# Attention and a gated feed-forward layer on one core: first loads and scores by pairs of heads, wider first products for half of batch 0, a last copy in two halves

## The chip, the cores and the metric

The kernel runs on one core of a Trainium2 chip. The metric is the time of one execution on the device in microseconds (us), lower being better. A core has five engines that work side by side and wait for each other by semaphores: TensorE (PE, matrix products; PEld is its loading of weights), ScalarE (ACT, functions element by element), VectorE (DVE), GpSimd (POOL, which here issues the loads) and SyncE (SP, which issues stores). Loads go to SBUF, the on-chip memory; products are written to PSUM, from where ACT and DVE read them.

## The reference

```python
# q, k, v: batch 8, heads 12, sequence 448, head dimension 64
scores = (1.0 / np.sqrt(64)) * np.matmul(q, k.transpose(0, 1, 3, 2))
scores = scores - np.max(scores, axis=-1, keepdims=True)
attn = np.exp(scores)
attn = attn / (np.sum(attn, axis=-1, keepdims=True) + 1e-09)
attn_out = np.matmul(attn, v).astype(np.float32)
x = attn_out.transpose(0, 2, 1, 3).reshape(3584, 768)
h = x @ w_in                              # w_in: 768 x 2048
g = h * (1.0 / (1.0 + np.exp(-h)))
out = (g @ w_out).astype(np.float32)      # w_out: 2048 x 768
```

So each of the 96 heads gives attention over 448 tokens, and the 3584 rows of 768 that come out go through two products with a gate between them.

## The kernel before

**Work and its tiling.** The heads of a batch are taken in three groups of four; a *unit* is one batch and one group, 24 in all, and units 0 to 2 are batch 0. A unit's keys and queries are loaded with partition = 32 x head + token block (`load_k` L314, `load_q` L319) and turned on DVE into the layout that PE wants (`turn_k` L375 with three transpositions, `turn_q` L392). Scores (`scores` L449, `score` L438) are products with 32 rows of PE for each head, so that the four heads of a unit run on PE's four groups of rows at once. They land in PSUM tiles `s`, each for two heads (y = 0 or 1), of which there are three. ACT exponentiates each tile (`expo` L479; L483 for the first two bursts of unit 0, L494 for all others). A unit's scores come in three or four *bursts*; each burst is two exponentials of 896 columns. Value products (L544, L558) and sums of exponentials give the attention, which is scaled on DVE into `xT` (L650, L661).

**The feed-forward layer.** First products `h` = `w_in` x `xT` (`ffn1` L684, all products in `times` L673), one block of 128 of the 2048 inner columns at a time, then a tanh on ACT (L705) and the gate on DVE (L740, L749). For batch 0 the first products are made in two pieces of 224 tokens (PIECES), two blocks sharing a PSUM tile. Second products `o` and `p` follow, for most tiles in a scheme with seven products instead of eight (`product` L910, `combine_g` L895); copies on ACT (`take_copy` L976) and sums on DVE (`take_sum` L981) bring them to SBUF, and `store` (L956) sends them out.

**What sets the order.** Nothing on the engines decides it: a planner in the kernel (`Order` L111, and the loop at L1880) plays the engines through with a cost for each operation and writes the instructions of every engine in the order that it finds. Its inputs are estimates: of products (`mm` L30), of ACT (`act` L34), of loads (L197 to L208, with an extra `DMA_SLOW` for one load). `qk_seq` (L1599) lists the score bursts in order, `qk_at` (L1620) says when the next may run, `run_qk` (L1644) places it; `av_seq` lists the value products; `moe` lists the feed-forward products, which fill PE in between. Before the first of those, idle time of PE is filled with products on zeros (`run_zeros` L1867): an opening run of FIRST = 47 columns-of-128, then shorter ones. POOL issues loads in the order of L1039 to L1066: keys of unit 0, queries of unit 0 in two pieces of columns, keys and queries of unit 1, keys of unit 2, V of batch 0, and so on. A buffer ring holds them back: there are two tiles for keys, so that the keys of unit 2 wait for the turn of unit 0's. An issue also waits until the eighth load before it has landed.

The lines of the order that matter here:

```python
plan_k(0, 0)
plan_q(0)
plan_k(0, 1)
plan_q(1)
plan_k(0, 2)
plan_v(0, 0, NG)
```

Of the kernel before, what the change touches and what calls it, by code (L numbers as in the profile page):

```python
# [18 lines left out]
PE_OUT = 0.20  # L19
# [91 lines left out]
class Order:  # L111
# [48 lines left out]
    def step(self):  # L160
# [26 lines left out]
        elif self.pool:  # L187
# [9 lines left out]
            if at is not None and at <= self.now:  # L197
# [5 lines left out]
                took += DMA_SLOW if len(self.sent) == 3 else 0.0  # L203
                few = len(self.sent) < 7
# [10 lines left out]
def kernel(  # L215
# [27 lines left out]
    PACE = 2.6  # L243
    NPL = 4
# [3 lines left out]
    COLD, FIRST, QUIET = 8.5, 47, 0.16  # L248
# [65 lines left out]
    def load_k(b, hg):  # L314
        t = sb.tile([128, TPP * D], FP16, name=f"rk_{b}_{hg}", tag="rk", bufs=NRK)
        nc.gpsimd.dma_start(out=t, in_=group_of(k, b, hg))
        rawk[(b, hg)] = t

    def load_q(n, g0, g1):  # L319
        b, hg = units[n][:2]  # L320
        if g0 == 0:
            rawq[n] = sb.tile([128, TPP * D], FP16, name=f"rq_{n}", tag="rq", bufs=NRQ)
        cols = slice(D * g0, D * g1)
        nc.gpsimd.dma_start(out=rawq[n][:, cols], in_=group_of(q, b, hg)[:, cols])  # L324
# [50 lines left out]
    def turn_k(b, hg):  # L375
        t = rawk[(b, hg)][:].bitcast(FP32).rearrange("p (g i) -> p g i", i=32)
        kt = sb.tile([128, TPP, 32, 2], FP16, name=f"KT_{b}_{hg}", tag="KT", bufs=3)
        KT[(b, hg)] = kt
        pairs = kt.rearrange("p g i e -> p (g i e)").bitcast(FP32)
# [3 lines left out]
        for x in (0, 2):  # L383
# [4 lines left out]
            if count == 4:  # L388
                lone = 12 * (not high)
                nc.vector.transpose(out=pairs[:, lone : lone + 2], in_=toks[:, :, 3 - 3 * at])  # L390

    def turn_q(n, g0, g1):  # L392
        t = rawq[n][:].bitcast(FP32).rearrange("p (g i) -> p g i", i=32)[:, g0:g1]
# [55 lines left out]
    def scores(n, w, ys):  # L449
        score_banks(n, w, ys)  # L450
        for c, q0, q1, at in strips_of(n, w):
            for e in range(2):
                for h in range(HG):
# [230 lines left out]
    def ffn1(b, f, t0, t1, strips, c0, c1):  # L684
        i = f % blocks(b)
# [13 lines left out]
    def blocks(b):  # L699
        return 2 if b == 0 else 1  # L700

    def tanh(b, f, t0, t1):
        n = (t1 - t0) * blocks(b)
# [30 lines left out]
    def gate(b, f, t0, t1):  # L734
        r = b % 2
        cut = 6 * 128 - S if b == 1 else S
        for lo, hi, dst, at in ((0, cut, G, S * r), (cut, S, X, -cut)):
            lo, hi = max(lo, t0), min(hi, t1)
            if b == 0 and lo < hi:
# [236 lines left out]
    def take_copy(qd, m):  # L976
        nc.scalar.copy(out=ost(qd, *OUT[m]), in_=bank(qd, BANK[m]))  # L977
        if m == 4:
            store(qd, *OUT[m])
# [25 lines left out]
    def plan_q(n):  # L1005
        ld_q[n] = [
            od.load(
                128,
                2 * D * (g1 - g0),
                lambda g0=g0, g1=g1: load_q(n, g0, g1),  # L1010
                None if g0 else rq_ring,
            )
            for g0, g1 in (PIECES if n == 0 else ((0, TPP),))
        ]
# [24 lines left out]
    plan_k(0, 0)  # L1039
    plan_q(0)  # L1040
# [35 lines left out]

    def plan_turn(n):
        b, hg, g0, g1 = units[n]
        if b == B - 1 and not rq_ring.can(1, od.now):
            return False  # L1080
        if (b, hg) not in kt_op:
            if not kt_ring.can(1, od.now):
# [4 lines left out]
                    "DVE", 0.73, lambda: turn_k(b, hg), [ld_k[(b, hg)]], 20, then=rk_ring.give  # L1087
                )
            )
        if b == B - 1:  # L1090
            rq_ring.take()
        qt_op[n] = [
# [3 lines left out]
                    0.13 + (g1 - g0) / 30.0,  # L1096
                    lambda g0=g0, g1=g1: turn_q(n, g0, g1),
                    [load],
                    20,
                    then=rq_ring.give if b == B - 1 else None,  # L1100
                )
            )
            for load, (g0, g1) in zip(ld_q[n], PIECES if n == 0 else ((0, TPP),))
        ]
        return True
# [32 lines left out]
    def gates_at(t, f):  # L1138
# [3 lines left out]
        for b in {(128 * t + c) // S for c in (0, 127)}:  # L1142
            x = g_op.get((b, f), [])
            made += x if len(x) >= (len(PIECES) if b == 0 else 1) else [None]
        return made

    def queue_ffn1(b, g0, g1):
        t0, t1, parts = 32 * g0, 32 * g1, []
        begun = {}
        for f in range(NFF) if b == 0 else [x for f in range(HF if b < PB else FILL) for x in (f, f + HF)]:  # L1150

          half = 6 if b else NDC
          for c0 in range(0, NDC, half):

            def run(f=f, c0=c0):
                c1 = c0 + half
                strips = b > 0 and od.mode == "cols" and bool(qk_seq or av_seq)
                op = Op("PE", half * mm(t1 - t0), lambda: ffn1(b, f, t0, t1, strips, c0, c1), tail=PE_OUT)
                if warm["on"]:
                    warm["on"] = False  # L1160
                n = blocks(b)
# [27 lines left out]
            def deps(f=f, c0=c0):  # L1189
                if c0:  # L1190
                    return [] if begun.get(f) == c0 else [None]
                if f % blocks(b) and f - 1 not in parts:
# [776 lines left out]
```

## Time and profile before

| | |
|---|---|
| three timed runs | 380.28, 380.77, 381.61 us; median 380.77 |
| the profiled execution | 380.37 us |
| its span (first to last instruction) | 378.6 us, so 1.8 us lie around it |
| PE busy, share of the span | 372.4 us, 98% |
| DVE, ACT, POOL busy | 269.7, 255.5, 84.9 us |
| granted clock of PE | full speed throughout |
| exponentials of 896 columns (L494) | 164, mean 923 ns |
| first products of 224 columns | 180 + 11 records, of 192 |
| last copy (L977, 128x384) | starts at 374.73, 0.48 us |

The profile is of one execution. Times inside it are microseconds from its first instruction. A group of rows in the timeline reads: start, duration, engine, line, operation, output<-inputs, shape, how many, and in brackets how long the engine sat idle before it and what ended that. In the chain of waits each row is a stretch of the path that ended last. A few records of products are missing from the trace. In the listing of loads "us to landing" is from issue to landing.

### The profile page before, as it was taken

The numbers are of one execution on the slowest core, as the hardware profiler recorded it, in microseconds if no ns is written. First come the engines' busy times: TensorE is split into PE (matmuls) and PEld (weight loads), VectorE is DVE, ScalarE is ACT, GpSimd is POOL, SyncE is SP. The second block draws the span as 40 slices with busy tenths as digits, with TensorE's granted clock in tenths as the row PEclk, the third lists the DMA queues.
The fourth block names the chain that finished last, engine by engine and source line by source line (L and its number), as shares of the span: only waits on it lengthen the run. The fifth ranks groups of instructions, "written<-read, shape, count | busy, mean of one in ns | idle before, by whom it ended". The sixth has DMA issues, their size and how long they took to land.

```text
span 378.6 us, 9949 instructions
## 1 busy us (share of the span) xinstructions
PE 372.4 (98%) x4024; PEld 191.5 (51%) x4024; DVE 269.7 (71%) x553; ACT 255.5 (67%) x400; POOL 84.9 (22%) x155
## 2 busy tenths in 40 slices
PE   7999999999999999999999999999999999999995
PEld 3367664444444444444444454545555555556663
DVE  3666859899995869995969998898475424446541
ACT  4988874897768787877788777658872238882221
POOL 6652438451007326006423200000000000000000
PEclk9999999999999999999999999999999999999999
DMA  7999999946139948148955421200002331002343
GB/s 120 191 208 210 206 204 186 190 53 98 17 92 124 184 49 124 26 94 116 170 86 73 54 53 34 68 18 0 3 1 59 94 74 26 0 2 59 84 110 83
DMA packets 35854, 34.47 MB, mean 91 GB/s; under 512 B 11872, under 2 KB 35040, under 8 KB 35808
## 3 DMA queue, kind: packets, MB, share of 16 engines
q0 software_dynamic: 25312, 22.82, 40.3%
q1 hardware_dynamic: 10080, 10.53, 10.6%
q8 instruction: 31, 0.51, 0.5%
q10 hardware_dynamic: 416, 0.49, 0.4%
q14 instruction: 15, 0.12, 0.1%
HBM read 45.61 MB, written 11.01 MB: 150 GB/s over the span
## 4 chain that ended last, share of the span: by engine, by line
PE 97%; DMA 1%; ACT 1%; DVE 0%; issue 0%; POOLq 0%
PE p L673 32%; PE h L673 21%; PE f L673 16%; PE s L438 12%; PE a L558 8%; PE o L673 3%; PE a L544 2%; PE a L591 2%; DMA rk<-in_k_dram 1%; ACT T L483 1%; PE z L1872 0%; PE z L673 0%; PE z L544 0%; DVE KT L387 0%; ACT ost L977 0%
## 5 line engine op out<-in xcount | busy, mean ns | idle before, releaser
L494 ACT ACTIVATE E<-s 128x896 f16<-128x896 f32 x164 | 142.0, 923 | 23.7 <-PE s L438 23.6
L673 PEld LDWEIGHTS <-w_in_t 128*128 128x128 f16 (+1 forms) x981 | 61.3, 97 | 45.2 <-issue 8.4
L673 PE MATMUL h<-xT,w_in_t 128*32 128x448 f16 (+2 forms) x834 | 84.0, 333 | 0.0
L344 POOL DMA_DIRECT2D V<-in_v_dram x88 | 48.4, 557 | 52.5 <-PE a L558 32.2
L673 PEld LDWEIGHTS <-G 128*128 128x128 f16 (+1 forms) x637 | 43.4, 97 | 32.4 <-issue 5.2
L977 ACT COPY ost<-p 128x384 f32<-128x384 f32 x52 | 24.9, 479 | 50.4 <-PE p L673 31.9
L705 ACT ACTIVATE th<-h 128x448 f16<-128x448 f32 x67 | 36.6, 546 | 22.8 <-PE h L673 19.1
L673 PE MATMUL p<-w_out_t,G 128*128 128x384 f16 (+1 forms) x343 | 51.9, 326 | 0.0
L438 PE MATMUL s<-rq,KT 32*128 32x448 f16 (+3 forms) x728 | 45.4, 347 | 1.3 <-DVE rq L402 1.0
L983 DVE TENSOR_TENSOR ost<-p,ost 128x384 f32<-128x384 f32 x39 | 21.6, 553 | 31.3 <-PE p L673 14.3
L673 PEld LDWEIGHTS <-S 128*128 128x128 f16 (+1 forms) x330 | 29.5, 98 | 23.5 <-issue 4.2
L673 PE MATMUL p<-D,S 128*128 128x384 f16 (+1 forms) x214 | 37.5, 326 | 0.0
L558 PE MATMUL a<-E,V 128*32 128x448 f16 (+1 forms) x640 | 32.9, 356 | 0.0
L749 DVE SCALAR_TENSOR_TENSOR G<-th,h 128x448 f16<-128x448 f16 (+1 forms) x52 | 28.8, 565 | 4.5 <-ACT th L705 3.9
L324 POOL DMA_DIRECT2D rq<-in_q_dram x25 | 13.8, 553 | 67.3 <-PE s L438 57.7
L661 DVE SCALAR_TENSOR_TENSOR xT<-a,rdn 128x448 f16<-128x448 f32 x46 | 27.0, 618 | 2.7 <-PE a L558 2.0
L438 PEld LDWEIGHTS <-KT 32*128 32x128 f16 (+1 forms) x824 | 12.5, 96 | 30.3 <-issue 28.1
L507 DVE TENSOR_TENSOR T<-T,E 128x1792 f16<-128x1792 f16 x20 | 21.7, 1086 | 3.9 <-ACT E L494 3.8
L876 DVE TENSOR_TENSOR p<-f,p 128x448 f32<-128x448 f32 x15 | 9.4, 624 | 20.4 <-PE f L673 13.5
L673 PE MATMUL f<-sx,tw 128*128 128x448 f16 x102 | 23.5, 352 | 0.0
L507 DVE TENSOR_TENSOR T<-E,E 128x1792 f16<-128x1792 f16 x20 | 21.6, 1082 | 2.5 <-ACT E L494 2.5
L558 PEld LDWEIGHTS <-V 128*32 128x32 f16 (+1 forms) x640 | 13.7, 95 | 18.0 <-issue 10.3
(95 smaller groups left out, 430.2 us busy)
## 6 DMA issues: line engine op xcount, KB each, us to landing
out_dram<-ost SPq DMA_DIRECT2D x194, 48.0 KB, 1.6
rk<-in_k_dram POOLq DMA_DIRECT2D x24, 224.0 KB, 5.0
rq<-in_q_dram POOLq DMA_DIRECT2D x23, 224.0 KB, 5.6
w_out_t<-in_moe_w_out_dram POOLq DMA_DIRECT2D x4, 768.0 KB, 12.5
V<-in_v_dram POOLq DMA_DIRECT2D x42, 64.0 KB, 4.1
V<-in_v_dram POOLq DMA_DIRECT2D x42, 48.0 KB, 4.3
w_in_t<-in_moe_w_in_dram POOLq DMA_DIRECT2D x6, 256.0 KB, 9.0
w_in_t<-in_moe_w_in_dram POOLq DMA_DIRECT2D x3, 512.0 KB, 12.3
```

The costliest lines, as they stand in the source:

```text
L324: nc.gpsimd.dma_start(out=rawq[n][:, cols], in_=group_of(q, b, hg)[:, cols])
L344: nc.gpsimd.dma_start(out=VT[b][32 * x : 32 * (x + 1), hs, at : at + count, :], in_=v[b, hs].rearrange("h (i g) d -> i h g d", g=TPP)[:, : ...
L438: nc.tensor.matmul(out=pS[p0 : p0 + 32 * (x1 - x0), h % 2, at : at + q1 - q0], lhsT=KT[(b, hg)][32 * h : 32 * (h + 1), key_rows(b, hg, c, ...
L494: nc.scalar.activation(out=E[(n, w)][:, 2 * y : 2 * y + 2, :], in_=pS_t[(n, w, y)][:, :, 0:S], func=AF.Exp, scale=attn_scale,)
L507: nc.vector.tensor_tensor(out=T[n], in0=T[n] if step else E[(n, 0)], in1=E[(n, step + 1)], op=ALU.add,)
L558: nc.tensor.matmul(out=a[32 * h : 32 * (h + 1), 0:S], lhsT=VT[b][k0:k1, HG * hg + h, place(b, hg, c), part - 1 :: 2], rhs=e[k0:k1, h], sta ...
L661: nc.vector.scalar_tensor_tensor(out=x3(b, cc)[:, cc % 3, 32 * g0 : 32 * g1], in0=acc[(n, part)][:, 0:nq], scalar=0.5, in1=rdn_t[n].rearra ...
L673: nc.tensor.matmul(out=out[i : i + cut], lhsT=w[:, i : i + cut], rhs=x, start=start, stop=stop, skip_group_check=True,)
L705: nc.scalar.activation(out=th, in_=h_t[(b, f, t0)][:, 0:n], func=AF.Tanh)
L749: nc.vector.scalar_tensor_tensor(out=dst[:, f, at + lo : at + hi], in0=th_t[(b, f, t0)][:, lo - t0 : hi - t0], scalar=1.0, in1=h_t[(b, f, ...
L977: nc.scalar.copy(out=ost(qd, *OUT[m]), in_=bank(qd, BANK[m]))
L983: nc.vector.tensor_tensor(out=t, in0=bank(qd, BANK[m]), in1=t, op=ALU.add)
```

## The change

Four edits, and a few constants of the planner.

- **Loads by pairs of heads.** Keys and queries of unit 0 come in halves of 64 partitions: keys of heads 0 and 1, queries of heads 0 and 1, keys of heads 2 and 3, queries of heads 2 and 3. Before, the keys came whole and the queries in two halves of the columns. One load is added. The turns on DVE go the same way: three operations and two query pieces for each pair of heads.
- **Scores likewise.** The first three bursts of unit 0 are split: all three for heads 0 and 1, then all three for heads 2 and 3. Each half burst is eight products on two of PE's four groups of rows.
- **Half of batch 0's first products 448 wide.** Blocks 0 to 7 stay in two pieces of 224 tokens, two blocks to a PSUM tile; blocks 8 to 15 are made in one piece of 448, one block to a tile. 96 products of 224 become 48 of 448.
- **The last copy by two engines.** Of the last tile of 384 columns ACT copies the first 192 and DVE the other 192.
- **The planner.** The extra for a slow load falls on the fourth load and no longer on the third; the opening run of dummies is 40 columns-of-128 for 47; turns for units 1 to 3 are urgent; a first product costs at least 0.0972. In `turn_k` one transposition is emitted last of the three where it was second.

The built order follows from the planner. In it, unit 0's first value product stands behind the last scores of unit 1 (it stood between unit 1's second and last scores), with dummy products of 1024 columns in its old place. First products and second products of batches 0 and 1 are shifted against the scores. From the scores of unit 11 on, about 110 us in the trace of before, PE has the same order as before. DVE's half of the last copy waits on ACT's semaphore, at the count that ACT's half sets.

The core of the diff:

```diff
-                took += DMA_SLOW if len(self.sent) == 3 else 0.0
-                few = len(self.sent) < 7
+                took += DMA_SLOW if len(self.sent) == 4 else 0.0
+                few = len(self.sent) < 8
...
+    BF0 = 8
...
-    COLD, FIRST, QUIET = 8.5, 47, 0.16
+    COLD, FIRST, QUIET = 8.5, 40, 0.16
...
-    def load_k(b, hg):
-        t = sb.tile([128, TPP * D], FP16, name=f"rk_{b}_{hg}", tag="rk", bufs=NRK)
-        nc.gpsimd.dma_start(out=t, in_=group_of(k, b, hg))
-        rawk[(b, hg)] = t
-
-    def load_q(n, g0, g1):
+    def load_k(b, hg, h0=0, h1=HG):
+        if h0 == 0:
+            rawk[(b, hg)] = sb.tile([128, TPP * D], FP16, name=f"rk_{b}_{hg}", tag="rk", bufs=NRK)
+        rows = slice(32 * h0, 32 * h1)
+        nc.gpsimd.dma_start(out=rawk[(b, hg)][rows], in_=group_of(k, b, hg)[rows])
+
+    def load_q(n, h0=0, h1=HG):
...
-        if g0 == 0:
+        if h0 == 0:
...
-        cols = slice(D * g0, D * g1)
-        nc.gpsimd.dma_start(out=rawq[n][:, cols], in_=group_of(q, b, hg)[:, cols])
+        rows = slice(32 * h0, 32 * h1)
+        nc.gpsimd.dma_start(out=rawq[n][rows], in_=group_of(q, b, hg)[rows])
...
-                nc.vector.transpose(out=pairs[:, lone : lone + 2], in_=toks[:, :, 3 - 3 * at])
-
-    def turn_q(n, g0, g1):
-        t = rawq[n][:].bitcast(FP32).rearrange("p (g i) -> p g i", i=32)[:, g0:g1]
+                lone = pairs[:, lone : lone + 2], toks[:, :, 3 - 3 * at]
+        nc.vector.transpose(out=lone[0], in_=lone[1])
+
+    def turn_q(n, g0, g1, h0=0, h1=HG):
+        rows = slice(32 * h0, 32 * h1)
+        t = rawq[n][rows].bitcast(FP32).rearrange("p (g i) -> p g i", i=32)[:, g0:g1]
...
-                for h in range(HG):
+                for h in [2 * y + i for y in ys for i in range(2)]:
...
-    def blocks(b):
-        return 2 if b == 0 else 1
+    def blocks(b, f):
+        return 2 if b == 0 and f < BF0 else 1
...
-        n = (t1 - t0) * blocks(b)
+        n = (t1 - t0) * blocks(b, f)
...
-        nc.scalar.copy(out=ost(qd, *OUT[m]), in_=bank(qd, BANK[m]))
+        t, p = ost(qd, *OUT[m]), bank(qd, BANK[m])
+        if (qd, m) == (LAST, 4):
+            nc.scalar.copy(out=t[:, 0 : OH // 2], in_=p[:, 0 : OH // 2])
+            nc.vector.tensor_copy(out=t[:, OH // 2 : OH], in_=p[:, OH // 2 : OH])
+        else:
+            nc.scalar.copy(out=t, in_=p)
...
-    plan_k(0, 0)
-    plan_q(0)
+    first_ld = {}
+    for i in range(2):
+        for fn, ring, x in ((load_k, rk_ring, (0, 0)), (load_q, rq_ring, (0,))):
+            first_ld[(i, fn)] = od.load(
+                64,
+                2 * D * TPP,
+                lambda fn=fn, x=x, i=i: fn(*x, 2 * i, 2 * i + 2),
+                None if i else ring,
+            )
...
+    def turn_bias(n):
+        return -11 if n <= 3 else 20
+
...
+        if n == 0:
+            plan_first_turns()
...
-                    "DVE", 0.73, lambda: turn_k(b, hg), [ld_k[(b, hg)]], 20, then=rk_ring.give
+                    "DVE", 0.73, lambda: turn_k(b, hg), [ld_k[(b, hg)]], turn_bias(n), then=rk_ring.give
...
+        if n:
+            plan_turn_q(n)
+        return True
+
+    def plan_turn_q(n):
...
-                    0.13 + (g1 - g0) / 30.0,
-                    lambda g0=g0, g1=g1: turn_q(n, g0, g1),
-                    [load],
-                    20,
-                    then=rq_ring.give if b == B - 1 else None,
+                    0.13 + TPP / 30.0,
+                    lambda: turn_q(n, 0, TPP),
+                    ld_q[n],
+                    turn_bias(n),
+                    then=rq_ring.give if units[n][0] == B - 1 else None,
...
-            for load, (g0, g1) in zip(ld_q[n], PIECES if n == 0 else ((0, TPP),))
...
-        return True
+
+    def plan_first_turns():
+        kt_ring.take()
+        for i in range(2):
+            heads = (2 * i, 2 * i + 2)
+            fn = lambda heads=heads: turn_k(0, 0, *heads)
+            then = rk_ring.give if i else None
+            kt_op[("half", i)] = od.add(
+                Op("DVE", 0.73, fn, [first_ld[(i, load_k)]], 18 + i, then=then)
+            )
+            for x, (g0, g1) in enumerate(PIECES):
+                fn = lambda heads=heads, g0=g0, g1=g1: turn_q(0, g0, g1, *heads)
+                op = Op("DVE", 0.13 + (g1 - g0) / 30.0, fn, [first_ld[(i, load_q)]], 18 + i)
+                qt_op[("half", i, x)] = od.add(op)
+        kt_op[(0, 0)] = kt_op[("half", 1)]
+        qt_op[0] = [qt_op[("half", i, x)] for i in range(2) for x in range(2)]
...
-            made += x if len(x) >= (len(PIECES) if b == 0 else 1) else [None]
+            made += x if len(x) >= blocks(b, f) else [None]
...
-        for f in range(NFF) if b == 0 else [x for f in range(HF if b < PB else FILL) for x in (f, f + HF)]:
+        for f in range(BF0 * (g1 - g0 == TPP), NFF if g1 - g0 == TPP else BF0) if b == 0 else [x for f in range(HF if b < PB else FILL) for x in (f, f + HF)]:
...
-                qk_seq += [([n], w, (0, 1)) for w in range(len(BURSTS[n]))]
+                if n == 0:
+                    qk_seq += [([0], w, (y,)) for y in range(2) for w in range(3)]
+                    qk_seq.append(([0], 3, (0, 1)))
+                else:
+                    qk_seq += [([n], w, (0, 1)) for w in range(len(BURSTS[n]))]
...
-            for x in {0 if c == NCH - 1 else i for c, i in BURSTS[n][c]} if n == 0 and c < 2 else ():
-                turns = [kt_op.get(units[0][:2]), *qt_op.get(0, [None] * 2)[x : x + 1]]
+            if n == 0 and c < NCH - 1:
+                y = ys[0]
+                turns = [kt_op.get(("half", y))]
+                turns += [qt_op.get(("half", y, x)) for x in {i for _, i in BURSTS[0][c]}]
```

## The prediction

> **What bounds the kernel now.** I read the page first, then the chain of waits of the first 80 us, then the timeline of the first 24 us engine by engine, then the end. The page says which engine it is:
>
> ```profile
> span 378.6 us, 9949 instructions
> PE 372.4 (98%) x4024; PEld 191.5 (51%) x4024; DVE 269.7 (71%) x553; ACT 255.5 (67%) x400; POOL 84.9 (22%) x155
> PE 97%; DMA 1%; ACT 1%; DVE 0%; issue 0%; POOLq 0%
> ```
>
> TensorE (PE) is busy 98% of the span and the chain lies on it for 97%. Only the first microseconds and the last four are anybody else's. But "busy" counts the dummy products on zeros and products that stand waiting inside a group, so the first 24 us need the timeline. The chain of waits opens so:
>
> ```profile
> 1.25 3.77 DMA rk<-in_k_dram
> ...
> 5.55 0.26 DVE KT L387
> 5.81 0.30 DVE rq L402
> 6.11 0.04 issue
> 6.15 0.63 PE s L438 x16
> 6.78 2.52 ACT T L483 x3
> ```
>
> The reader sees a start bound by one load: all keys of unit 0 land at 5.02, are turned on DVE, half the queries after them, and the first exponential starts at 6.76. Then the timeline, PE and ACT rows picked out:
>
> ```profile
> 9.85 0.65 DVE L402 STREAM_TRANSPOSE rq<-rq 128x448 f32<-128x448 f32 x1 [0.34 <-DMA rq<-in_q_dram]
> 9.97 9.86 ACT L494 ACTIVATE E<-s 128x896 f16<-128x896 f32 x12
> ...
> 13.96 0.82 PE L438 MATMUL s<-rq,KT 32*128 32x448 f16 x8
> 14.71 0.56 PE L544 MATMUL a<-T,V 128*32 128x448 f16 x8
> ...
> 15.58 0.81 PE L438 MATMUL s<-rq,KT 32*128 32x448 f16 x8
> 16.33 0.56 PE L544 MATMUL a<-T,V 128*32 128x448 f16 x8
> ...
> 17.28 0.74 PE L438 MATMUL s<-rq,KT 32*128 32x224 f16 x16
> ...
> 20.34 2.53 ACT L494 ACTIVATE E<-s 128x896 f16<-128x896 f32 x3 [0.51 <-PE s L438]
> ```
>
> ACT runs without a gap from 6.76 to 19.83, one exponential each 0.80 us. Up to about 17 us ACT sets the pace: the scores of unit 1 (13.96, 15.58) follow each other by two exponentials, 1.6 us, and the 0.87 us between them is filled with a value product (14.71). From 17.28 the roles change: PE has no gap, and ACT waits for it (0.51 at 20.34). After 24 us the groups on PE follow without any stall, and past 110 us the changed program has the same order on every engine but the last copy. So **what counts is when PE gets through unit 2's scores, how much PE work follows, and the last copy.** The end:
>
> ```profile
> 374.73 0.48 ACT L977 COPY ost<-p 128x384 f32<-128x384 f32 x1 [4.72 <-PE p L673]
> 375.24 0.50 ACTq L970 DMA_DIRECT2D out_dram<-ost  x1
> ```
>
> **The change part by part.**
>
> *First exponential.* Landings before: keys 5.02 (issued 1.25, 3.77), first query piece 5.5 (1.93 + 3.6), second 6.9 (2.47 + 4.4), next keys 8.7 (2.99 + 5.7), next queries 9.8 (3.51 + 6.3), then 10.9. A load of 224 KB thus takes 1.1 us of the stream, one of 112 KB about 0.5. After: the first half of the keys lands near 4.5, that of the queries near 5.0. The key turn (three operations, 5.04 to 5.81) takes 0.76, a query piece 0.37; rows are not columns, so 64 partitions take as long. Queries turned at 5.6, scores 0.6 (6.15 to 6.76 before), **first exponential near 6.15: 0.6 earlier.** The scores of a pair of heads use half of PE's rows, so eight products take as long (0.5) as sixteen did: 1.5 us more PE for unit 0. It is covered: before 12.3 us PE held 41 dummy columns-of-128 between the scores, now 29. DVE gets five operations more (about 1.5 us) and has 3.4 idle of the 7 us from 5 to 12. The second half has to give exponential 4 at 6.15 + 3 x 0.80 = 8.55; with queries landing at 6.9, turned at 7.3, scored by 7.95, it does.
>
> *What is late next.* Exponential 7 (11.56 before) needs the queries of unit 1: landing 9.83, turned 9.85 to 10.50. The bytes ahead of them are the same. Scores of 64 rows from 10.55, two rounds of 0.19 and some 0.2 until ACT starts: 11.15, where the chain alone would allow 10.95. So of 0.6 only **0.4** is left. Bounds: 0.62, if that load comes 0.2 earlier; -0.1, if the extra DMA issue costs a half load's 0.5. I keep 0.41, since the stream moves the same bytes.
>
> *POOL.* Keys of unit 2 wait for the second key turn: issued near 7.0 instead of 6.10, the four V loads behind them 0.8 later. Loads from there on take 4.8 to 6.1 us to land where the first took 3.8, so they queue behind data, and this is hidden; without that cover V would come 0.8 later, and its first reader now stands 1.2 us later.
>
> *The moved value product.* The order of the changed program puts unit 0's first value product (14.71 before) behind unit 1's last scores; dummies fill its place. ACT still sets when those scores may run: 16.33 less 0.41. Then both value products (0.87 each) must pass before unit 2's scores. PE loses 0.87; it regains 0.09 (scores at 17.28 waited for a query turn) and 0.16 (group of 0.67 that needs 0.51). **Front: +0.87 - 0.25 - 0.41 = +0.2** (0.0 to +0.7). PE is the bound from there, so it stays.
>
> *First products 448 wide.* In the chain, 30 products of 224 take 2.98 and 24 take 2.41: 0.095 each; 12 of 448 take 2.38, of which 0.11 is the change of form: 0.189. So 96 x 0.0958 - 48 x 0.189 = 0.12; the mean of all 224 pitches, 0.097, gives 0.24. I take **-0.15**. Tanh and gates stay as many and as long.
>
> *Forms.* From unit 2's first scores to the point where the orders meet PE changes form 77 times before, 75 after. Eight scores take 0.505 where two rounds need 0.38, a group of first products 0.106 over its products: 0.11 each, **-0.22** (0 to -0.25).
>
> *Last copy.* The built order shows VectorE's half waiting for ACT's half. A copy of 384 takes 0.479, of 448 about 0.53, so 192 on ACT 0.33; VectorE's half from its sum of 384 (0.558) and its 224 against 448 columns (0.417, 0.62) 0.36; from one to the other 0.03. 0.72 instead of 0.48: **+0.24** (side by side it would be -0.1). Both stores wait for it; nothing hides it. The Trainium skill, "PSUM — Partial Sum Buffer", section on PSUM bank collisions, says that two engines must not read one bank at once; by it such a split has to be serial, as the order is.
>
> **Sum:** +0.2 - 0.15 - 0.22 + 0.24 = **+0.1** on the profiled execution's 380.37 (span 378.6 and 1.8 around it): 380.5. The three timed runs have a median of 380.77, 0.4 above that execution; 380.5 lies between.
>
> **The rivals.**
>
> *Faster.* The first 0.6 reach PE whole and the moved product costs nothing (the stalls of 0.25 to 0.29 in unit 1's three score groups take it up): -0.6 - 0.37 + 0.24 = -0.75, 379.6; with the last copy side by side 379.3. For it: those stalls exist. Against: they are waits on ACT's pace, which the change leaves at 0.80. Beyond 0.3% needs a little more still: 0.15.
>
> *Slower: half loads that take as long as whole ones.* If rows 0 to 63 alone get half the rate, four half loads cost 0.55 more each, the queries of unit 1 land at 12.0, exponential 7 starts 1.8 after its old time, and the total is +2.3: 382.7. It decides from a landing about 1.0 later than 9.83. Against: the V loads write 32 partitions each, and the first, 192 KB issued at 6.62, lands at 11.9, 1.0 after the load before it, the rate of 128 partitions. The Trainium skill, "SBUF — State Buffer", section "Door 1: The DMA port swizzle", says that partitions 0 to 63 reach only 8 of 16 ports; by that rule this rival's way is open, and the trace's V loads speak against it. 0.07.
>
> *Slower: PE still slow at the first scores.* Dummy products of 512 columns follow each other by 0.43 until 3.9 and by 0.22 after, and the opening run shrinks from 47 to 40 columns-of-128. Were PE slow until 10 us, six half groups at 0.9 and the dummies would push unit 1's scores by some 1.5: 382. Against: the step came after 2.9 us of work, and 40 still last 3.6. 0.07.
>
> **How the numbers follow.** A measurement of this kernel can tell 0.3%, 1.14 us, from no change. Forecast and what lies within that: 0.70; faster by more 0.16 (the rival and what I don't see); slower by more 0.14 (both slow rivals). Range: the front's bounds (-0.2 to +0.5 about my value), the last copy's (-0.35), the forms' (+0.22), and the spread of the runs (-0.5 to +0.8 about their median): 379.6 to 381.5, which leaves about 2 in 10 out.
>
> **What would show it.** First exponential at 6.1 to 6.2; exponential 7 near 11.15, just after the query turn; unit 2's scores at 17.4 to 17.7, no earlier than 17.28; first products 448 wide at 0.189; the last copy in two pieces one after the other, ending 0.7 after its start. Unit 2's scores before 17.0, or a stall on PE after 24 us, would make it wrong.

## The result, and the profile after

The changed kernel takes 383.0 us (median of 6 runs, 382.73 to 383.66), the kernel before 380.9 us in the same session (6 runs, 380.28 to 381.61): a ratio of 1.006, 95% interval 1.0049 to 1.0071. It is **slower by 2.1 us**, where no change was forecast.

The profiled execution took 382.92 us. The page of the changed kernel, with the lines that answer to those shown of before:

```profile
span 381.1 us, 9931 instructions
PE 373.5 (98%) x4015; PEld 187.6 (49%) x4015; DVE 271.6 (71%) x559; ACT 255.6 (67%) x400; POOL 85.4 (22%) x156
PEclk9699999999999999999999999999999999999999
PE 93%; DMA 2%; SPq 1%; POOL 1%; DVE 1%; issue 0%; ACT 0%; ACTq 0%; POOLq 0%
```

PE is still 98% busy, so the totals tell nothing. The chain says more: PE holds 93% of it where it held 97%, and DMA, POOL and SP's queue have come in. The second slice of PEclk (9.5 to 19 us) has a 6: PE was granted half its clock for a part of it, from 10.63 to 17.46 us. The chain of waits opens so (start, length, what):

```profile
3.99 6.44 DMA rq<-in_q_dram
10.43 0.02 issue
10.45 0.66 DVE rq L410
11.10 0.04 issue
11.15 0.97 PE s L446 x11
12.12 1.07 PE z L1923 x3
13.19 0.87 PE s L446 x8
14.05 1.61 PE z L552 x15
```

The start now hangs on the queries of unit 1, which land at 10.43 (9.83 before), and then on a PE with half its clock: 1.61 us for sums of exponentials that took 0.87. ACT's timeline shows what comes of it:

```profile
5.91 1.73 ACT L491 ACTIVATE T<-s 128x896 f16<-128x896 f32 x2 [3.88 <-PE s L446]
...
12.14 1.73 ACT L502 ACTIVATE E<-s 128x896 f16<-128x896 f32 x2 [0.97 <-PE s L446]
14.09 1.73 ACT L502 ACTIVATE E<-s 128x896 f16<-128x896 f32 x2 [0.22 <-PE s L446]
16.57 3.35 ACT L502 ACTIVATE E<-s 128x896 f16<-128x896 f32 x4 [0.76 <-PE s L446]
```

The first exponential is 0.86 earlier than before; the seventh (12.14) is 0.58 later, the eleventh (16.57) 1.81. The last copy, of ACT and of DVE:

```profile
377.04 0.32 ACT L987 COPY ost<-p 128x192 f32<-128x192 f32 x1 [4.72 <-PE p L681]
```

```profile
377.39 0.36 DVE L988 COPY ost<-p 128x192 f32<-128x192 f32 x1 [1.02 <-ACT ost L987]
```

The two halves stand one behind the other, 0.71 in all. And on PE there is a wait that the kernel before does not have, for a copy of ACT that itself waited for a store to land:

```profile
297.36 1.79 PE L681 MATMUL p<-w_out_t,G 128*128 128x384 f16 x10 [0.40 <-ACT ost L990]
```

Where exponentials of the same number stand in both traces, the difference adds up without a rest:

| part | predicted | measured in the profiled executions |
|---|---|---|
| front, to exponential 21 (23.93 before) | +0.2 | +2.22 |
| from there to exponential 93 (wide products, changes of form) | -0.37 | -0.46 |
| PE at 297 us | 0 | +0.56 |
| last copy | +0.24 | +0.23 |
| sum | +0.1 | +2.55 = 382.92 - 380.37 |

(From the products before 297 us to those behind, PE falls back by 0.56 more; 0.40 of it is the wait shown.) The terms of the middle and of the copy hold. The front was wrong by 2.0 us, and the stall was not foreseen.

### The profile page after: what moved, and what is told of

It reads as the page before. It is cut to its first block, busy times and chain, and to the rows that moved or that the text cites. A ratio compares the mean times of both kernels' runs of the same rounds, so it can differ in the third digit from the quotient of the medians.

```text
span 381.1 us, 9931 instructions
## 1 busy us (share of the span) xinstructions
PE 373.5 (98%) x4015; PEld 187.6 (49%) x4015; DVE 271.6 (71%) x559; ACT 255.6 (67%) x400; POOL 85.4 (22%) x156
## 3 DMA queue, kind: packets, MB, share of 16 engines
q1 hardware_dynamic: 10080, 10.53, 10.4%
## 4 chain that ended last, share of the span: by engine, by line
PE 93%; DMA 2%; SPq 1%; POOL 1%; DVE 1%; issue 0%; ACT 0%; ACTq 0%; POOLq 0%
PE p L681 29%; PE h L681 21%; PE f L681 16%; PE s L446 11%; PE a L566 8%; PE o L681 3%; PE a L552 2%; PE a L599 2%; DMA rq<-in_q_dram 2%; SPq L978 1%; PE z L552 1%; PE z L1923 1%; POOL rk L319 0%; DMA out_dram<-ost 0%; PE z L681 0%
## 5 line engine op out<-in xcount | busy, mean ns | idle before, releaser
L681 PEld LDWEIGHTS <-w_in_t 128*128 128x128 f16 (+1 forms) x933 | 56.8, 97 | 48.5 <-issue 8.4
L757 DVE SCALAR_TENSOR_TENSOR G<-th,h 128x448 f16<-128x448 f16 (+1 forms) x60 | 33.5, 571 | 4.7 <-ACT th L713 4.3
L566 PEld LDWEIGHTS <-V 128*32 128x32 f16 (+1 forms) x640 | 13.5, 95 | 18.1 <-issue 10.5
```

Of the source, the lines that this page charges most:

```text
L566: nc.tensor.matmul(out=a[32 * h : 32 * (h + 1), 0:S], lhsT=VT[b][k0:k1, HG * hg + h, place(b, hg, c), part - 1 :: 2], rhs=e[k0:k1, h], sta ...
L681: nc.tensor.matmul(out=out[i : i + cut], lhsT=w[:, i : i + cut], rhs=x, start=start, stop=stop, skip_group_check=True,)
L757: nc.vector.scalar_tensor_tensor(out=dst[:, f, at + lo : at + hi], in0=th_t[(b, f, t0)][:, lo - t0 : hi - t0], scalar=1.0, in1=h_t[(b, f, ...
```

## The experiments

Three theories of the front went in: the **queue of loads** (a slow third load, and a queue that runs dry because the keys of unit 2 are issued late), **PE's clock**, and the **moved value product**. "Lands" is the moment at which the last of the 16 DMA engines has raised the load's semaphore.

### Where the loss sits: control, wide_and_copy, front_alone

control is the changed kernel unchanged. wide_and_copy is the kernel before with `BF0 = 8` (and what hangs on it) and the split `take_copy`. front_alone is the changed kernel with

```diff
-    BF0 = 8
+    BF0 = 16
-        if (qd, m) == (LAST, 4):
+        if False:
```

> The changed kernel once more, for a trace in which PE has its full clock from 10 to 18 us (in the trace at hand it was granted about 0.5 there). Theory 1, the queue of loads: the queries of unit 1 land near 10.4 instead of 9.83, because the third half load is slow (it landed 1.6 us after the slower of the first two would let one expect) and the queue runs dry near 9 us; then exponential 7 stands at 11.7 or later with any clock, the exponentials 9 to 15 late by 0.8 or more, and the time is 383 again. Theory 2, PE's clock: with the full clock the groups of scores take 0.75 and not 0.86, the sums of exponentials 0.87 and not 1.62, the first attention products stand less than 1 us behind those of before, and the time of a run with the full clock is 381.7 or less. Theory 3, the moved value product alone: exponentials 7 to 13 on time to 0.2, and then 0.9 lost in one step before the scores of unit 2.

> The kernel before with the two edits that do not touch the first 20 us: half of batch 0's first products 448 wide, the last copy by two engines. If the loss is in the front (theories 1 to 3) this is 380.9 - 0.15 to -0.45 for the products and the changed forms, +0.23 for the copy: 380.5 to 381.0, that is no change. Rival: the wide products hold PE up later (a tanh of one block too late, a full ring) and part of the 2.1 us is theirs: 382 or more.

> The changed kernel with all of batch 0's first products 224 wide again and the last copy on ACT alone: loads, turns and scores by pairs of heads are left. If the loss is in the front, first attention products 2.2 us late as in the changed kernel, and 383.0 to 383.3 (2.2 on 380.9, and 0.2 either way for the order of the middle). Rival: the wide products lose it: 381.

Measured, against 380.63 for before: control 382.77 (ratio 1.005, interval 1.0032 to 1.0067), wide_and_copy 380.89 (1.0006, 0.9994 to 1.0017), front_alone 382.36 (1.005, 1.0032 to 1.0068). The loss is in the loads and scores by pairs. control's trace has the full clock throughout from 4.92 us, so **PE's clock is not the cause**: the time is the same without the dip, and the five other runs of the changed kernel above, 382.73 to 383.66, have a mean clock of 0.999 or 1.0. Its exponentials 7 to 14 are 0.54 *earlier* than before: up to 16.6 nothing is lost here. Then the gain goes at once, 1.9 us by exponential 21. (Some 0.85 of this is the moved value product of the prediction: keys_spare below loses as much at the same place, with no load late.) ACT and PE of control:

```profile
10.23 7.41 ACT L502 ACTIVATE E<-s 128x896 f16<-128x896 f32 x9
18.90 1.73 ACT L502 ACTIVATE E<-s 128x896 f16<-128x896 f32 x2 [1.26 <-PE s L446]
```

```profile
16.65 0.56 PE L552 MATMUL z<-T,V 128*32 128x448 f16 x8 [0.82 <-DMA V<-in_v_dram]
...
18.29 0.58 PE L446 MATMUL s<-rq,KT 32*128 32x224 f16 x16
```

PE waits 0.82 us for the values, and the scores of unit 2 start at 18.29 (17.28 before). Two things end there together: the value products that came late, and the turn of unit 2's queries (17.58 to 18.23). Exponential 21 is 1.37 late, and another 0.4 is a wait for `w_out`, a load further down the same queue:

```profile
PE o L681 <- DMA w_out_t<-in_moe_w_out_dram: 0.4, 1, 0.4
```

The chain of waits of control says why those are late:

```profile
2.43 4.44 DMA rk<-in_k_dram
6.87 0.02 issue
6.89 0.64 DVE KT L393 x2
7.53 0.13 DVE KT L397
7.66 0.31 DVE rq L410
7.96 0.52 POOL rk L319
8.48 1.79 POOL V L346 x3
10.28 0.04 issue
10.32 0.60 POOL V L346
10.92 6.64 DMA rq<-in_q_dram
17.56 0.29 issue
17.85 9.96 DMA w_in_t<-in_moe_w_in_dram
```

Read it from the top: the third load (keys of heads 2 and 3) lands at 6.87; DVE turns it and a query piece, and with that the first keys' tile is free; only then does POOL issue the keys of unit 2 (7.95 for 6.10 before), the four loads of values behind them, and the queries of unit 2 (10.92 for 9.07), which land at 17.56. From there the chain stays on the queue, over loads of weights, until `w_out` lands at 58.05: in this trace it is the late queue that sets the end, and not the place of exponential 21. In the meantime the queue had run dry, which the GB/s row of the first 25 us shows (0.625 us a slice; before, then control):

```profile
GB/s 0 0 0 0 54 149 181 184 152 133 182 184 192 198 190 190 160 167 166 149 185 204 219 198 218 204 215 197 175 203 202 208 205 206 202 202 208 223 199 208
```

```profile
GB/s 0 0 0 0 60 175 164 98 75 129 169 172 169 192 95 80 120 187 188 168 172 147 147 172 200 189 230 189 213 193 205 200 208 203 205 200 210 203 213 193
```

Two dips: 98 and 75 at 4.4 to 5.6 us (the third load), 95 and 80 at 8.75 to 10 us. In the second the earlier loads start their last packet at 9.17, and the first packets of the keys of unit 2, 1.2 us after their issue, are slow (up to 1.2 us each, where 0.15 is usual). The queries of unit 1 are not late here, 9.61.

### The third half load: halves_only

The kernel before with its first four loads as in the changed kernel, turns and scores whole:

```diff
-    plan_k(0, 0)
-    plan_q(0)
+    first_k, ld_q[0] = [], []
+    for i in range(2):
+        first_k.append(od.load(64, 2 * D * TPP, lambda i=i: load_k(0, 0, 2 * i, 2 * i + 2), None if i else rk_ring))
+        ld_q[0].append(od.load(64, 2 * D * TPP, lambda i=i: load_q(0, 2 * i, 2 * i + 2), None if i else rq_ring))
```

> The kernel before with unit 0's loads in four half loads of 64 partitions, but its turns and scores whole, so that DVE turns nothing until the third half load has landed, and PE runs dummies for longer. What is asked is where the third half load lands. Theory 1a, DVE's turns of the first half (4.2 to 5.5 us) slow the writes of the load beside them: without them it lands near 5.3 instead of 6.86, the queries of unit 1 near 9.7 or sooner. Theory 1b, the third load of a queue is slow by itself, whoever runs beside it (before, the third took 4.4 us to land, the first two 3.8 and 3.6): it lands at 6.5 to 7 again. The time follows the front: 380.5 to 382 by 1a, 382 or more by 1b.

It takes 383.79 (ratio 1.0078, 1.0059 to 1.0097): all turns now wait for the second pair, and the first exponential stands at 8.85. The third half load lands at 6.56 with no DVE operation beside it, so 1b holds: DVE does not slow it. In all 19 traces the second load lands 0.5 to 0.9 behind the first and the third, always of 112 KB, 0.9 to 2.4 behind the second. But the half loads are not free: in the 11 traces that have them the third comes 1.54 to 2.43 later (median 2.0) and the queries of unit 1 land at 9.61 to 11.04 (median 10.4); in the 8 without, 0.94 to 2.13 (1.4) and 9.24 to 10.22 (9.75). Why was not tried.

### The late keys by themselves: late_keys_1, late_keys_2

The kernel before, every engine but POOL with the same instructions in the same order (late_keys_1 clears once, late_keys_2 twice):

```diff
+        for _ in range(2 if (b, hg) == (0, 2) else 0):
+            nc.gpsimd.memset(t, 0.0)
         nc.gpsimd.dma_start(out=t, in_=group_of(k, b, hg))
```

> The kernel before, with nothing but a clearing of the keys' tile of unit 2 by POOL ahead of its load: every engine else has the same instructions in the same order, and that load and all behind it on POOL are issued later, by one clearing (about 1 us): near 7.0 instead of 6.10, which is where the prediction put them in the changed kernel. Prediction's view: the queue still holds the queries of unit 1 until 9.8, the issue is hidden, the keys of unit 2 land at 10.9 as before, time 380.6 to 381.0. Theory now (a load lands no earlier than 4.0 to 4.1 us after its issue, so the queue runs dry from an issue later than 6.8): landing near 11.0, loads behind it 0.1 to 0.3 late, hardly any change of the time.

> The same with two clearings, so that the keys of unit 2 are issued near 8.0, where the changed kernel has them (7.95). Theory now: they land near 12.0 instead of 10.9, the last values near 15.7 to 16.4 instead of 14.6, the queries of unit 2 near 17.0 instead of 15.7, the scores of unit 2 stand 0.5 to 1.3 late, and all of this comes out at the end: 381.3 to 382.3. Rival (the prediction's cover, or the cause lies in the scores by pairs of heads or in the moved value product): no change, 380.6 to 381.0, although the loads land later.

late_keys_2 takes 382.67 against 380.54 (1.005, 1.0031 to 1.0069): **a late issue, with none of the change in the kernel, costs as much by the medians as the whole change.** The size is loose: the six runs lie at 381.69 to 383.91, three of them with a mean clock of 0.993 to 0.996, and the profiled execution is the fastest, 1.3 late. late_keys_1, with the issue at 6.94, where the prediction had put it, takes 381.55 (1.0023, 1.0011 to 1.0036), more than either view expected. PE's waits in late_keys_2 (engine, line, waited for: total, times, longest):

```profile
PE a L546 <- DMA V<-in_v_dram: 1.5, 1, 1.5
```

late_keys_1 has the same line. There the keys of unit 2 land 0.4 late (11.31), but the second load of values follows the first by 2.14, not 1.17 (late_keys_2: 2.05): a stall of the stream adds itself, and the kernel before has no slack for it. So neither run shows the late issue quite alone. That POOL's clearing brings this stall is not excluded, though wide_alone below has one of 2.65 without it.

PE's first row of unit 2's scores in late_keys_2, which stand behind the late values:

```profile
18.71 0.77 PE L440 MATMUL s<-rq,KT 32*128 32x224 f16 x16
```

### Values ahead of the keys: v_first, v_first_one_copy, v_first_dummies, values_first

One line moved, in the changed kernel (v_first), with the last copy whole (v_first_one_copy), with more dummies in two gaps of PE (v_first_dummies), and in the kernel before (values_first):

```diff
-    plan_k(0, 2)
     plan_v(0, 0, NG)
+    plan_k(0, 2)
```

> The changed kernel with one line moved: the keys of unit 2 are loaded behind the values of batch 0 and no longer ahead of them, so that POOL does not stand before the values until the keys' tile is free; unit 0's first value product comes back between unit 1's scores with it. Theory now: the queue never runs dry, values land by 13.5 to 14.5 (16.4 in the changed kernel), the queries of unit 2 by 16 (17.5), no wait of PE for values, the scores of unit 2 at 16.8 to 17.5 instead of 18.3, and the time 381.0 to 381.8. Rival, the slow third half load alone: nothing is won, 382.8. A stall of 0.5 us of PE at 297 us, which the changed kernel has and the kernel before has not, may stay or go; it is not part of either theory.

> The same with the last copy on ACT alone again. The last copy is then 0.48 and not 0.71: 0.2 to 0.25 less than the kernel with the values first, 380.2 to 381.5 with what is open there. If the two halves side by side had been worth something, it would be slower instead.

> The kernel with values first and one last copy, with 14 and 9 columns-of-128 of dummy products more in the two gaps of PE that wait for the second pair's queries (7.2 to 8.2 us) and for the queries of unit 1 (10.5 to 11.0). Theory 2, narrowed: where PE idles in 7 to 11 us its clock is sometimes taken back to half for one or two stretches of 3.4 us; that, and not the loads, makes half of that kernel's runs 381.6 to 384.3 instead of 380.5. With the gaps filled the clock stays, all runs lie at 380.3 to 381.0, median 380.6. Rival: the clock is lost whatever PE does in the gaps, or the slow runs have another cause: the same spread, median 381.9.

> The kernel before with one line moved: the keys of unit 2 loaded behind the values of batch 0, as in the changed kernel with the values first. POOL then never stands before a free queue, and the values have 1.1 us in hand (landing 13.5 instead of 14.6), so that a stall of the stream of 1 us (the values of other traces landed at 15.3 to 16.1 in kernels with the loads of before) no longer reaches PE. Theory, the values' landing is the thin cover of the kernel before: same median or up to 0.3 less, 380.2 to 380.5, and a narrower spread than 380.0 to 382.3. Rival, the queries of unit 1 or 2 are the thin cover (10.4 to 11.0 in the two kernels with values first): 381 or more, as there at the full clock.

| kernel | median us | ratio, interval |
|---|---|---|
| v_first | 382.86 | 1.005, 1.003 to 1.007 |
| v_first_one_copy | 381.92 | 1.0032, 1.0011 to 1.0052 |
| v_first_dummies | 381.38 | 1.0033, 1.0016 to 1.005 |
| values_first | 381.87 | 1.0042, 1.0028 to 1.0056 |

As a test of the front this failed, since the line moves more than a load. values_first has every load early (queries of unit 2 at 15.56) and still loses 1.6: the planner puts two normalisations on DVE ahead of the turn of those queries, which ends at 18.4, and PE's scores wait for it (PE, then DVE):

```profile
18.46 0.58 PE L438 MATMUL s<-rq,KT 32*128 32x224 f16 x16 [0.35 <-DVE rq L402]
```

```profile
16.05 1.16 DVE L661 SCALAR_TENSOR_TENSOR xT<-a,rdn 128x448 f16<-128x448 f32 x2
...
17.80 0.60 DVE L402 STREAM_TRANSPOSE rq<-rq 128x448 f32<-128x448 f32 x1
```

They did show the clock's price. v_first_one_copy has five runs with a mean granted clock of 0.998 or more, at 380.45 to 380.73, and seven with 0.991 to 0.996, at 381.6 to 384.33. Busy time of PE by stretches, v_first_one_copy and then v_first_dummies (stretch, us, busy and operations, granted clock, DMA share, GB/s):

```profile
7.00:11.00 4.00, 2.44 (x26) 1.00 1.15 168
11.20:14.60 3.40, 3.40 (x31) 0.50 1.38 201
```

```profile
7.00:11.00 4.00, 4.00 (x37) 1.00 1.03 138
11.20:14.60 3.40, 3.13 (x46) 1.00 1.40 199
```

Where PE was busy 2.44 of 4 us, the next 3.4 us ran at half the clock; with the gaps filled it kept it, and so did all 12 runs of v_first_dummies (0.998 to 1.0). Their median is not the 380.6 of the theory: the queries of unit 1 land at 10.82 there. Ten of the 12 lie at 381.19 to 381.95; 382.47 and 385.21 at the full clock are not explained. So the second theory is right about most of the spread, and is no cause of the changed kernel's median.

### The wait for the buffer alone: keys_spare and its kin

The keys of unit 2 go into the ring of the queries, which has a free tile of the same size. POOL then issues them and the values at 4.50 to 7.13 without a wait for the first keys' turn, and PE's order is that of the changed kernel but for a few dummies:

```diff
-            rawk[(b, hg)] = sb.tile([128, TPP * D], FP16, name=f"rk_{b}_{hg}", tag="rk", bufs=NRK)
+            tag, bufs = ("rq", NRQ) if (b, hg) == (0, 2) else ("rk", NRK)
+            rawk[(b, hg)] = sb.tile([128, TPP * D], FP16, name=f"rk_{b}_{hg}", tag=tag, bufs=bufs)
...
-        ld_k[(b, hg)] = od.load(128, 2 * D * TPP, lambda: load_k(b, hg), rk_ring)
+        ld_k[(b, hg)] = od.load(128, 2 * D * TPP, lambda: load_k(b, hg), rq_ring if (b, hg) == (0, 2) else rk_ring)
```

keys_spare_one_copy also has the last copy whole; keys_spare_before and keys_spare_before_wide are the same edit in the kernel before, without and with `BF0 = 8`.

> The changed kernel with the keys of unit 2 loaded into a buffer of the queries' ring (four tiles of the same size, one free then) and no longer into that of unit 0's keys: POOL issues them and the values at once, with no wait for the key turn of the second pair, and PE's order is that of the changed kernel but for a few dummies. Theory (late issue): the keys of unit 2 land near 10.7 instead of 12.0, the values by 14.5 to 15 instead of 16.4, the queries of unit 2 by 16 instead of 17.6; PE does not wait for values; the scores of unit 2 stand at 17.3 or sooner, and the time falls by 1.0 to 1.8 on the changed kernel's 382.8: 381.0 to 381.8, of which 0.5 may be the stall at 297 and 0.23 the last copy. Rival (scores by pairs, moved value product or the half loads as such): 382.5 or more.

> The same with the last copy on ACT alone: 0.2 to 0.25 less than with the copy in two halves, and so 380.7 to 381.6; the best that the changed front can give so far.

> The kernel before with the same one edit, unit 0's loads and scores whole. Its keys of unit 2 wait from 4.0 to 6.1 for a buffer, and land at 10.9, where the queue would have them at 10.9 in any case: no change of the landings, 380.3 to 380.6. What it may win: no second start of POOL's issuing, and so none of the stalls of about 1 us that the stream showed some 1.25 us after POOL began to issue again (7.9 and 9.2, 7.5 and 8.7, 6.9 and 8.2); then the values land at 14.5 in every run and the spread narrows, 380.1 to 380.4.

> The same with half of batch 0's first products 448 wide: 0 to 0.25 less than without, 380.0 to 380.5. The best of all if the wide products gain what the prediction gave them.

All four against 380.56: keys_spare 381.65 (1.0031, 1.002 to 1.0043), keys_spare_one_copy 380.90 (1.001, 0.9999 to 1.0022), keys_spare_before 380.57 (1.0001, 0.9992 to 1.0009), keys_spare_before_wide 380.26 (0.9993, 0.9985 to 1.0002). (One of the 12 runs of keys_spare_before took 2104.57 us, which is not explained; it hardly moves the median.) The theory holds: with one tile's place the loss against before falls from 2.1 to 1.1 us. PE's waits in keys_spare have no line for values any more, and unit 2's scores stand at 17.54:

```profile
PE p L682 <- ACT ost L991: 0.9, 1, 0.9
PE s L447 <- DVE rq L411: 0.2, 1, 0.2
```

```profile
17.54 0.58 PE L447 MATMUL s<-rq,KT 32*128 32x224 f16 x16
```

The landings side by side (us):

| | before | control | late_keys_2 | keys_spare |
|---|---|---|---|---|
| keys of unit 2 issued | 6.10 | 7.95 | 7.93 | 4.50 |
| queries of unit 1 land | 9.83 | 9.61 | 9.94 | 9.81 |
| keys of unit 2 land | 10.90 | 12.02 | 11.79 | 10.90 |
| last values land | 14.62 | 16.40 | 16.36 | 14.51 |
| queries of unit 2 land | 15.72 | 17.56 | 17.45 | 15.65 |
| PE waits for values | 0 | 0.82 | 1.50 | 0 |
| scores of unit 2 start | 17.28 | 18.29 | 18.71 | 17.54 |
| exponential 21, against before | 0 | +1.37 | +1.46 | +0.46 |

What is left in keys_spare's profiled execution (1.28) is the prediction's sum and one term more: front +0.46, middle -0.46, PE's wait at 296 us +1.03 (0.87 of it the wait shown), last copy +0.23. The wide products are worth 0.3 (380.57 to 380.26), the whole copy 0.75 here, more than the 0.23 of the trace; keys_spare has eight runs alone, two of them with a clock of 0.991 and 0.995, and the rest of the 0.75 is not explained. No version is faster than before by more than the interval allows; keys_spare_before_wide comes nearest.

### The wide products alone: wide_alone

The kernel before with `BF0 = 8` and nothing else.

> The kernel before with half of batch 0's first products 448 wide and nothing else, for the term of the prediction (-0.15 for the products): 380.2 to 380.5, and less by 0.2 to 0.25 than the kernel that had the last copy in two halves as well (380.89), if that copy is in series as predicted. If the wide products gain nothing, 380.5 to 380.7.

380.62 against 380.48 (1.0003, 0.9994 to 1.0011): nothing gained, as the rival had it. Its profiled execution (381.47) is the slowest of its runs: the second load of values was 2.65 behind the first and PE waited 1.3 for it. The same edit gained 0.3 where the keys' wait was gone. In that one execution the stall outweighed it; whether stalls hid it in the other runs is not shown.

### The wait at 297 us: small_dummies, keys_spare_small

The changed kernel, and keys_spare_one_copy, with the opening run in smaller pieces:

```diff
-                n, wide = FIRST, 4
+                n, wide = FIRST, 1
```

> The changed kernel with the opening run of 40 columns-of-128 on PE issued as 40 products of 128 columns and no longer as 10 of 512: the same work on zeros, 60 PE instructions more (30 products, 30 weight loads), every later instruction in the same order. It bears on one thing, the 0.5 us that PE waits at 297 us in the changed kernel. In its traces a packet of 8 KB or more in the queue of instructions stands at 290.9 and 291.4, in the midst of a burst of stores, and SP's next store is held 1.8 us there. Theory, fetching of PE's code: 60 instructions more move that fetch some 5 us earlier (they come every 21 us), ahead of the burst at 288.6, the wait goes, and the time falls by 0.4 to 0.6, to 382.1 to 382.5. Rival, the wait belongs to the order of work there: it stays, 382.8.

> The kernel of keys_spare_one_copy with its opening run of dummies as 40 products of 128 columns for 10 of 512: 60 PE instructions more, the same work. In keys_spare_one_copy PE waits 0.8 us at 296 us, a packet in the queue of instructions stands at 290.4 in the burst of stores that begins at 288.1, and SP's next store is held 2.1 us. Theory, fetching of PE's code: the packet moves ahead of the burst (285 to 286), the wait goes, and with it 0.5 to 0.9 us: 380.0 to 380.4. Rival, the wait belongs to the order of work: 380.9 again.

In both traces the packet of the queue of instructions moved as expected (from 290.9 to 285.5 and from 290.4 to 286.3, ahead of the burst of stores), and the wait is gone. So it is in front_alone, whose packet stands at 285.7. PE of small_dummies goes through in one piece there:

```profile
295.69 2.60 PE L681 MATMUL p<-w_out_t,G 128*128 128x384 f16 x15
```

The medians do not show the price: 382.68 (1.0059, 1.0043 to 1.0076) and 381.99 (1.003, 1.0014 to 1.0047), with half of the runs short of the full clock (a mean of 0.989 to 0.997). In the profiled execution of keys_spare_small PE had its full clock only from 13.82 us; that of small_dummies has a new wait of 0.97 at 30.11, for a gate on DVE. So the mechanism is supported by the place of the packet, its worth only by the traces (a wait of 0.4 to 0.9 us).

## Why the prediction was wrong

- **First exponential.** Right in direction, somewhat better: 5.91 and 5.99 in the changed kernel (6.15 predicted), 6.35 in keys_spare, where the clock came up later (6.33).
- **What is late next.** Right in control and keys_spare alone: there the queries of unit 1 land at 9.61 and 9.81, and exponential 7 of control stands at 11.03 (11.15 predicted). "The bytes ahead of them are the same", but they do not come as fast: the median of the 11 traces with half loads is 10.4, 0.6 later than without, and 10.43 in the profiled execution of the changed kernel.
- **POOL: the step that failed.** "They queue behind data, and this is hidden." Two things were wrong in it. The issue was put at 7.0 and came at 7.95, since the third load lands 2.1 us behind the second, at 6.87, and its turn and a query piece come before POOL goes on. The prediction's "about 0.5" for a load of 112 KB was one of two gaps in its own rows; the other, from 5.54 to 6.91, was 1.37. And the cover was taken as the queue's depth, when what counts is how soon a load can land after its issue: 3.9 to 4.1 us in the traces where the queue was running out (7.93 to 11.79, 7.95 to 12.02), 3.4 to 3.9 for the 224 KB that begin the kernel before. The queue's next free place was 9.61 + 1.1 = 10.7. So 1.3 us of the stream were lost in control, and every load behind was late by it and more (the last values by 1.78, the queries of unit 2 by 1.84). The prediction priced the values ("V would come 0.8 later") and set them off against a later reader; it left out the queries of unit 2 behind them, the load that its own front hung on, and `w_out` behind those. Its sign was unit 2's scores at 17.4 to 17.7: they stood at 19.67 in the changed kernel's first trace, 18.29 in control, and 17.54 with the wait gone. By the medians this step is worth 1.0 of the 2.1. Here a rule would have misled further: the Trainium skill, "DMA: Bandwidth & Descriptors", section "Anatomy of one DMA — SWDGE (gpsimd) path", fits a load at 2.0 us plus its bytes at 436 KB a us. An estimate from that page is 2.5 us for 224 KB, a landing at 10.5, and a hidden issue; the traces say 3.9 to 4.1.
- **The moved value product, wide products, forms.** Held within bounds: with the wait gone the front is +0.46 (+0.2, bounds 0 to 0.7), the moved product taking 0.85 where 0.62 was reckoned, and the middle -0.46 (-0.37).
- **Last copy.** Held: in series, +0.23 (+0.24).
- **No stall after 24 us.** The second step that failed: PE falls back by 0.56 and 0.67 at 297 in the changed kernel's two traces, and by 1.03 in keys_spare.
- **Rivals.** The time that came is that of the two slow rivals (382.7 and 382), by neither mechanism. Half loads to 64 partitions do not take as long as whole ones: the second half load follows the first by 0.51 and 0.54, as 112 KB to 128 partitions did before (0.52). That is some 215 GB/s, as for whole loads (224 KB each 1.1 us), so that partitions 0 to 63 do not halve the rate of this stream; whether they would halve a faster one, no run shows. A slow PE was there in one trace, and did not set the time.

## What to carry to other kernels

When a change delays an issue, follow that queue to its end: a late load shifts all that is issued behind it, and each reader that has no slack, here of the values, of the next queries, and of `w_out` 40 us on, can set the price. Cover for a late issue is the time at which the queue runs dry less the least time from issue to landing, taken from a load that found the queue running out, and not the bytes that still wait. A buffer that becomes free later because its reader was split is such a delay; one spare tile elsewhere undid it here.

## What the runs showed of the hardware

- **The stream stumbles, often soon after POOL starts to issue again.** Packets of 0.7 to 1.2 us (0.15 is usual for their size) came in clusters some 1.25 us after the first issue behind a wait: issue at 6.94, cluster from 8.2; 7.47 and 8.7; 7.72 and 9.0; 7.95 and 9.2. In the kernel before, whose queue was full then (issue at 6.10), there is none. It is not the only case: keys_spare_one_copy has such packets from 7.1 to 9.5 without that wait, and its queries of unit 1 land at 10.55. A cause was not tried.
- **PE's clock goes by stretches of 3.41 us.** It was lost for 3.41 or 6.83 us at a time, and came up between 3.7 and 6.9 us in 18 of 19 traces. The Trainium skill, "TensorE: Matmul & The Clock Gate", section "Part 1: The HAM clock gate (the "warmup" mystery)", tells of a free-running window of about 3.4 us; the lengths agree. That page has the clock fall after an idle window; here a stretch in which PE was busy 2.44 of 4 us was enough. Of the two traces with dummies of 128 columns for 512, the clock came up at 6.61 in one and at 13.82 only in the other.
- **Fetching of code can hold up stores.** In the 16 traces where a 16 KB packet of the queue of instructions stands amid this burst of stores, at 286.9 to 297.0, a gap of 0.8 to 2.2 us in SP's issues (0.4 to 0.5 is usual) begins within 0.6 us of it; in the four where PE waits 0.4 us or more behind it, the gap is 1.7 to 2.2. A gap of 2.1 stands without such a packet too (front_alone, at 295.68). Adding 60 PE instructions at the start moved the packet 4 to 5 us earlier, 280 us on, and a wait of 0.5 and 0.8 us of PE went with it in the trace. That the packet is PE's code is inferred from this.
